# RWKV-6 attention and an erf-gated MLP on one core: products of near tokens over blocks of 16 instead of 8

## The chip, the cores and the metric

The kernel runs on one core of a Trainium2 chip. A core has TensorE (matmul), VectorE, ScalarE, GpSimd and SyncE; in the profile they are PE (and PEld, the loading of weights), DVE, ACT, POOL and SP. The metric is the device time of one execution in microseconds (us), the median of several runs. The profile is of one further execution; its span is 635.4 us.

## The reference

Everything is float32. The first half is a recurrent attention over batch 4, 8 heads, 768 tokens and head size 48:

```python
for t in range(S):
    kt, vt, rt, wt = (k[:, :, t], v[:, :, t], r[:, :, t], w[:, :, t])
    cur = np.einsum('bhd,bhe->bhde', u[None] * kt, vt)
    y[:, :, t] = np.einsum('bhd,bhde->bhe', rt, state + cur)
    state = wt[:, :, :, None] * state + np.einsum('bhd,bhe->bhde', kt, vt)
```

So token t reads token s < t with the weight sum over d of r[t] * k[s] * w[s+1] * ... * w[t-1], and itself with r * u * k. The heads' outputs, side by side, are the 3072 x 384 input x of the second half:

```python
h = x @ w_in                                  # 384 -> 2048
sp = np.maximum(h, 0.0) + np.log1p(np.exp(-np.abs(h)))
g = h * erf(sp)
return (g @ w_out).astype(np.float32)         # 2048 -> 384
```

## The kernel before

**Steps.** The tokens go through in 12 steps. A step handles 128 tokens of two batch entries, all 8 heads: 16 pairs of head and batch entry, in chunks of 64 tokens (HC = 64, two chunks to a step). `attend` (line 350) is the attention of one step, `hidden` (L520) and `project` (L559) are the layers w_in and w_out of a step, cut into 8 pieces each. A piece of `project` is 4 matmuls of 384 columns (L568), a piece of `hidden` 6 of 256 columns (L547); each float32 matmul is two instructions in the profile. Step s runs its own attention beside `project` of step s-3 and `hidden` of step s-1. After step 11 only dense pieces are left.

**Levels.** Within a chunk of 64 tokens, pairs (s, t) are covered by six levels. Level n takes the pairs in which s lies in the left and t in the right half of a block of 2^n tokens. For a level, TensorE multiplies the columns of r and k of 32 blocks (L390) into the PSUM tile `pp`; then VectorE scales r and k in place by products of decays (`scale`, L226, the instruction at L231), so that the next level has the right decay between halves, and copies the level's pairs from `pp` into the matrix `own` (L409, a copy under a mask; at level six ScalarE does it, L416). Products of decays over blocks of 2, 4, ... tokens (`tots`) come from GpSimd (L306). The next level's matmuls wait for the scaling before them.

**After the levels.** TensorE multiplies `own` with v into y (L435, in two halves), transposes k (L446, which needs level six's scaling), and forms the chunk's update of the state (L464). VectorE adds it to the decayed state, which is `middle`, the state between the two chunks (L476); GpSimd decays that (L480) and VectorE makes the next state (L484). Then TensorE adds what y reads from the state and from `middle` (L498). ScalarE copies y into xT, the input of w_in, and the next step begins.

**Near tokens.** Steps 0 to 3 run all six levels on TensorE. From step 4 on (DIRECT = 4), levels one to three are replaced: `prepare(s)` (L235) computes all pairs within blocks of 8 tokens (NEAR = 8) by elementwise work. It needs r, k and w a second time, as rows: a partition holds a block of 8 tokens of two heads, 96 numbers per token. GpSimd multiplies, distance by distance (n = 0 to 7): terms[n] = r[n:] * k[:-n] (L296), and between two distances k is carried on by k *= w (L295). The terms lie in two rooms of SBUF, `front` and `back`. VectorE sums them over the head (L324), the sums go to DRAM and come back in the order of tokens (`by_blocks`, `by_tokens`), and VectorE puts them on the block diagonal of `own` (L342). The levels from four on then overwrite the rest.

**Order.** Every engine works in the order in which the program is written; the order is set by hand. `prepare` is a generator. During step s, `attend` advances the generator of step s+1 by `next(following)` after every level above NEAR_LOG, after the transposes and before the last place; in step 3, the first that prepares near tokens for a successor, this is so too:

```python
if level > (NEAR_LOG if s >= DIRECT - 1 else 1):
    next(following, None)
place(level - 1)
```

The first advance issues all products and the decay products on GpSimd; the third issues the sums and both DRAM transfers on VectorE and SyncE; the fourth and the rest the scalings one to three and `own`. `place` puts the dense pieces and the activations between the levels: `advance` (L585) issues the next of softplus (L529), erf (L532) and the multiplication h * erf (L536), `beside` (L594) the pieces. In step 3, two pieces go to each of eight places, `project` at the first four and `hidden` at the last four. From step 4 on there are five places with 4 and 4 pieces of `project` and 3, 3 and 2 of `hidden`. At the end of a step the inputs and the rows of step s+2 are loaded (`load_step`, `load_rows`). Steps 0 to 3 also convert the weights (`convert`).

Of the kernel before, what the change touches and what calls it, by code (L numbers as in the profile page):

```python
# [11 lines left out]
FP32 = mybir.dt.float32  # L12
# [3 lines left out]
ALU = mybir.AluOpType  # L16

P = 128
# [3 lines left out]
NJ = 2  # L22
# [11 lines left out]


DIRECT = 4
NEAR_LOG = 3
NEAR = 1 << NEAR_LOG
LOG = 6
MASKED = 5  # L40
# [2 lines left out]
def view(ap, offset, dims):  # L43

    return bass.AP(ap.tensor, ap.offset + offset, [ap.ap[0], *dims])
# [12 lines left out]
def kernel(  # L58
# [14 lines left out]
    nc = tc.nc  # L73
    PSUM = bass.MemoryType.PSUM

    n_steps, _, _, JP, C = rkw.shape
    NH, D = v.shape[2:]
# [9 lines left out]
    assert n_steps == SPC * n_pairs and NP == KT + 1 == 4 and NG == 2 and P // NEAR * NH // 2 == P  # L87
# [23 lines left out]
    first = const.tile([P, HC], FP32, name="first")  # L111
    block_sb = const.tile([P, HC], FP32, name="block_sb")

    sums = const.tile([P, NEAR, 2, NEAR], FP32, name="sums")
    u_row = const.tile([P, 2 * D], FP32, name="u_row")
# [110 lines left out]
    def scale(s, level):  # L226

        in_t, tots = loaded[s][0], ready[s][1]
        half, nb = 1 << (level - 1), JP * C >> level
        halves = view(in_t[:, 0:2], half, [[JP * C - half, 2], [2 * half, nb], [1, half]])  # L230
        nc.vector.tensor_mul(  # L231
            halves, halves, view(tots[level - 1], 0, [[1, 2], [2, nb], [0, half]])
        )

    def prepare(s):  # L235


        in_t = loaded[s][0]
        if s < DIRECT:
            rk1 = att.tile([P, 2, JP, C], FP32, name="rk1", bufs=1)  # L240
            parts = 1 if s else NJ
            def multiply_u(i, x):
                n = slice(i * JP // parts, (i + 1) * JP // parts)
                with_u, plain = (
                    [
                        t[:, x, n].rearrange("p n (t two) -> p n t two", two=2)[..., one]
                        for t in (rk1, in_t)
                    ]
                    for one in (x, 1 - x)
                )  # L250
                if not s and not x:
                    nc.vector.tensor_mul(
                        with_u[0], with_u[1],
                        u_sb[:, :, None].to_broadcast([P, NP, C // 2]),
                    )
                    nc.vector.tensor_copy(out=plain[0], in_=plain[1])
                    return
                for p in range(NP):
                    of = slice(p, None, NP)
                    nc.scalar.mul(  # L260
                        out=with_u[0][:, of], in_=with_u[1][:, of], mul=u_sb[:, p : p + 1]
                    )
                nc.scalar.copy(plain[0], plain[1])

            if s < 2:
                for i in range(parts):
                    for x in range(2):
                        multiply_u(i, x)
                yield
            else:  # L270
                yield
                yield
                multiply_u(0, 0)
        if s >= DIRECT:
# [4 lines left out]
            room = [front[:].rearrange("p x n t -> p (x n t)")] + [  # L279
                back[:].rearrange("p x n two -> p (x n two)").bitcast(FP32)  # L280
            ]
            terms = []
            for n in range(NEAR):
                if n in (0, 3):
                    free, used = room.pop(0), 0
                size = (NEAR - n) * 2 * D
                terms.append(free[:, used : used + size].rearrange("p (t n) -> p t n", n=2 * D))
                used += size
            nc.gpsimd.tensor_mul(  # L289
                terms[0], k, u_row[:, None, :].to_broadcast([P, NEAR, 2 * D])  # L290
            )
            nc.gpsimd.tensor_mul(terms[0], terms[0], r)
            for n in range(1, NEAR):
                if n > 1:
                    nc.gpsimd.tensor_mul(k[:, : NEAR - n], k[:, : NEAR - n], w[:, n - 1 : NEAR - 1])  # L295
                nc.gpsimd.tensor_mul(terms[n], r[:, n:], k[:, : NEAR - n])  # L296

        tots, tot = [], in_t[:, 2].rearrange("p n t -> p (n t)")
        tot_sb = att.tile([P, JP * (C - NC)], FP32, name="tot_sb")
        used = 0  # L300
        for level in range(1, LOG + 1):
            tots.append(tot)
            nb = JP * C >> level
            new = tot_sb[:, used : used + nb]
            pair = tot.rearrange("p (n two) -> p n two", two=2)
            nc.gpsimd.tensor_mul(new, pair[:, :, 0], pair[:, :, 1])  # L306
            tot = new
            used += nb
            if level == 2 and s < DIRECT:
                yield  # L310
        if s < DIRECT:
            ready[s] = rk1, tots, tot
            yield
            if s >= 2:
                yield
                multiply_u(0, 1)
            return

        own = att.tile([P, NH, HC], FP32, name="own")
        ready[s] = own, tots, tot  # L320
        yield
        yield
        for n in range(NEAR):
            nc.vector.tensor_reduce(  # L324
                out=view(sums[:], n, [[2 * NEAR + 1, NEAR - n], [NEAR, 2]]),
                in_=terms[n].rearrange("p t (n d) -> p t n d", d=D),
                axis=mybir.AxisListType.X, op=ALU.add,
            )
        by_blocks = dram.tile([P, NEAR, 2 * NEAR], FP32, name="by_blocks")
        nc.sync.dma_start(out=by_blocks[:], in_=sums[:].rearrange("p s n t -> p s (n t)"))  # L330
        by_tokens = att.tile([P, NH, NEAR], FP32, name="by_tokens", bufs=1)
        nc.sync.dma_start(
            out=by_tokens[:].rearrange("p (g n) t -> p g (n t)", n=2),
            in_=by_blocks[:].rearrange("(g b) s n -> (b s) g n", g=NH // 2),
        )
# [13 lines left out]

    def attend(s, xT, place, behind):  # L350
# [243 lines left out]
    def beside(s, k):  # L594


        kind, of, pieces = (projs, s - 3, 2) if k < 4 else (hids, s - 1, 2)
        if s >= DIRECT:
            kind, of = (projs, s - 3) if k < 2 else (hids, s - 1)
            pieces = (4, 4, 3, 3, 2)[k]  # L600
        if s in ALONE:
            kind, of, pieces = hids, s - 1, 1
        if not 0 <= of < n_steps:
# [3 lines left out]
        for _ in range(pieces):  # L607
            next(kind[of])


    CONVERT = (
# [13 lines left out]
    with tc.manual_schedule(  # L625
# [19 lines left out]
        for s in range(n_steps):  # L645
            xTs[s] = xs.tile([P, KT, UNIT], FP32, name="xT")
            places = iter(range(8))

            def convert_at(n):
                if s < len(CONVERT) and n < len(CONVERT[s]):  # L650
                    for what in CONVERT[s][n]:
                        conversion.send(what)

            def place(n):
                if s in ALONE:
                    convert_at(n)
                    advance(ALONE[s][n])
                else:
                    advance()
                    convert_at(n)  # L660
                beside(s, next(places))

            attend(s, xTs[s], place, lambda: convert_at(LOG + 2))
            if s + 2 < n_steps:
                load_step(s + 2)
                if s + 2 >= DIRECT:
# [101 lines left out]
```

## Time and profile before

The median of three runs is 637.16 us (637.15 to 637.78).

| engine | busy us | share of the span | instructions |
|---|---|---|---|
| PE | 622.5 | 98% | 7338 |
| PEld | 458.2 | 72% | 7338 |
| DVE | 306.9 | 48% | 311 |
| ACT | 301.3 | 47% | 374 |
| POOL | 276.1 | 43% | 240 |

A group of instructions in the profile is read as: source line, engine, operation, output <- input by the program's names, shapes, count | busy us in all, mean ns of one | us that the engine sat idle just before, and what ended most of that. A row of the timeline is: start in us, length in us, then the same names; "x64" says that 64 instructions are merged. In brackets stands the idle time before it and what released it. A group of matmuls that overlap has a mean of one that is longer than its share of the busy time: 2816 instructions of L390 with a mean of 214 ns take 46.5 us in all. The TensorE clock that the throttle granted is 1.00 throughout.

In the steps from 4 to 10 the three compute engines beside TensorE have time left: in the step from 207.23 to 256.10 us, VectorE is busy for 24.8 us, ScalarE for 21.8 and GpSimd for 27.6 of 48.9.

### The profile page before, as it was taken

What the parts mean: (1) busy time and instruction counts of PE and PEld (TensorE: products, weight loads), DVE (VectorE), ACT (ScalarE), POOL (GpSimd) and SP (SyncE); (2) the same over time, 40 slices, a digit from 0 to 9 for tenths busy, and PEclk for the clock granted to TensorE, in tenths of its full rate; (3) what the DMA queues carried; (4) which work ended last, traced back from release to release, by engine and by line L of the source; (5) the groups of instructions that cost most, each with busy time, mean ns of one, the idle gap of its engine ahead of it and who ended that gap; (6) DMA issues with size and microseconds to landing.
All of it is one profiled execution on the core that took longest, in us unless ns stands there. A gap on an engine that the chain in (4) does not pass through costs nothing.

```text
span 635.4 us, 16193 instructions
## 1 busy us (share of the span) xinstructions
PE 622.5 (98%) x7338; PEld 458.2 (72%) x7338; DVE 306.9 (48%) x311; ACT 301.3 (47%) x374; POOL 276.1 (43%) x240
## 2 busy tenths in 40 slices
PE   8889999999999999999999999999999999999997
PEld 7567787678678678668668668768768758768654
DVE  4588597577346256266265365366446322011110
ACT  2537778756424544544534524624624625634520
POOL 4338175495194196097097087088079100000000
PEclk9999999999999999999999999999999999999999
DMA  8366371400500500500510410420330000000000
GB/s 326 130 241 201 136 260 56 200 15 10 206 26 10 207 26 9 206 26 10 183 49 10 168 65 9 152 81 9 103 128 11 8 13 14 7 23 3 1 25 25
DMA packets 24628, 53.84 MB, mean 85 GB/s; under 512 B 11376, under 2 KB 16752, under 8 KB 23152
## 3 DMA queue, kind: packets, MB, share of 16 engines
q1 hardware_dynamic: 23408, 52.23, 23.1%
q8 instruction: 57, 0.93, 0.6%
q10 hardware_dynamic: 1152, 0.59, 0.4%
q14 instruction: 11, 0.09, 0.1%
HBM read 46.39 MB, written 5.24 MB: 81 GB/s over the span
## 4 chain that ended last, share of the span: by engine, by line
PE 91%; DVE 3%; ACT 3%; issue 1%; DMA 1%; POOL 0%; SPq 0%; DVEq 0%; ACTq 0%
PE m L568 40%; PE m L547 38%; PE pp L390 6%; PE y L435 2%; PE pp L446 2%; PE y L498 2%; PE pp L464 2%; DVE in L231 1%; DMA in<-in_rkw 1%; ACT rk L260 1%; DVE own L409 1%; ACT own L416 0%; ACT rest L189 0%; ACT pp L187 0%; DMA xT<-y 0%
## 5 line engine op out<-in xcount | busy, mean ns | idle before, releaser
L547 PE MATMUL m<-xT,w_in_sb 128*128 128x256 f32 x1152 | 260.1, 382 | 0.6 <-DMA xT<-y 0.3
L568 PE MATMUL m<-w_out_sb,h 128*128 128x384 f32 x768 | 253.5, 489 | 0.0
L547 PEld LDWEIGHTS m<-xT,w_in_sb 128*128 128x128 f32 x1152 | 214.6, 190 | 33.2 <-issue 1.6
L568 PEld LDWEIGHTS m<-w_out_sb,h 128*128 128x128 f32 x768 | 144.2, 190 | 97.4
L231 DVE TENSOR_TENSOR in<-in,tot_sb 128x1024 f32<-128x1024 f32 x60 | 80.8, 1347 | 154.4 <-PE pp L390 153.2
L536 DVE TENSOR_TENSOR h<-h,sp 128x1024 f32<-128x1024 f32 x48 | 80.3, 1713 | 67.7 <-ACT sp L532 67.7
L554 ACT COPY h<-m 128x512 f32<-128x512 f32 x96 | 56.2, 586 | 104.2 <-PE m L547 104.0
L577 ACT COPY o<-m 128x384 f32<-128x384 f32 x24 | 11.5, 479 | 148.4 <-PE m L568 136.6
L289 POOL TENSOR_TENSOR rk<-words,u_row 128x768 f32<-128x768 f32 x8 | 17.3, 2157 | 124.8 <-DMA words<-in_rk_rows 124.8
L306 POOL TENSOR_TENSOR tot_sb<-tot_sb 128x256 f32<-128x256 f32 (+4 forms) x60 | 54.1, 902 | 4.5
L390 PEld LDWEIGHTS pp<-in 48*64 48x64 f32 (+1 forms) x2816 | 41.0, 127 | 20.5 <-issue 17.5
L295 POOL TENSOR_TENSOR words<-words,rest 128x576 f32<-128x576 f32 (+5 forms) x48 | 52.6, 1096 | 3.8
L390 PE MATMUL pp<-in 48*64 48x64 f32 (+1 forms) x2816 | 46.5, 214 | 4.2 <-DVE own L409 2.3
L532 ACT ACTIVATE sp<-sp 128x2048 f32<-128x2048 f32 x24 | 45.9, 1911 | 0.3
L529 ACT ACTIVATE sp<-h 128x2048 f32<-128x2048 f32 x24 | 45.9, 1911 | 0.3
L532 ACT ACT_TABLE_LOAD x24 | 30.8, 1283 | 20.4 <-issue 20.2
L296 POOL TENSOR_TENSOR words<-words 128x480 f32<-128x480 f32 (+4 forms) x40 | 32.8, 819 | 3.1
L529 ACT ACT_TABLE_LOAD x24 | 30.8, 1283 | 3.0 <-issue 2.6
L296 POOL TENSOR_TENSOR rk<-words 128x672 f32<-128x672 f32 (+1 forms) x16 | 31.9, 1994 | 0.6
L324 DVE TENSOR_REDUCE sums<-words 128x10 f32<-128x480 f32 (+4 forms) x40 | 17.7, 452 | 26.5 <-POOL words L296 25.9
L203 POOL TENSOR_TENSOR w_out_sb<-w_out_sb,rest 128x768 int32<-128x768 int32 x8 | 18.1, 2271 | 27.4 <-DVE w_out_sb L199 27.4
L476 DVE TENSOR_TENSOR middle<-faded,pp 48x384 f32<-48x384 f32 x20 | 11.0, 552 | 32.9 <-PE pp L464 32.6
(57 smaller groups left out, 427.2 us busy)
## 6 DMA issues: line engine op xcount, KB each, us to landing
in<-in_rkw SPq DMA_DIRECT2D x11, 1536.0 KB, 6.6
words<-in_moe_w_in SPq DMA_DIRECT2D x8, 768.0 KB, 6.0
words<-in_moe_w_out SPq DMA_DIRECT2D x8, 768.0 KB, 4.8
words<-in_rk_rows SPq DMA_DIRECT2D x8, 768.0 KB, 8.4
v<-in_v SPq DMA_DIRECT2D x12, 384.0 KB, 7.0
out<-o SPq DMA_DIRECT2D x24, 192.0 KB, 1.9
rest<-in_w_rows SPq DMA_DIRECT2D x8, 384.0 KB, 8.9
in<-in_rkw SPq DMA_DIRECT2D x2, 512.0 KB, 4.6
```

The costliest lines, as they stand in the source:

```text
L203: nc.gpsimd.tensor_tensor(out=into, in0=into, in1=rest[:], op=ALU.add)
L231: nc.vector.tensor_mul(halves, halves, view(tots[level - 1], 0, [[1, 2], [2, nb], [0, half]]))
L295: nc.gpsimd.tensor_mul(k[:, : NEAR - n], k[:, : NEAR - n], w[:, n - 1 : NEAR - 1])
L296: nc.gpsimd.tensor_mul(terms[n], r[:, n:], k[:, : NEAR - n])
L306: nc.gpsimd.tensor_mul(new, pair[:, :, 0], pair[:, :, 1])
L390: nc.tensor.matmul(pp[s0 : s0 + m, e, n, :m], lhsT=rk[rows(e), 1, n, s0 : s0 + m], rhs=rk[rows(e), 0, n, t0 : t0 + m], start=True, stop=True,)
L529: nc.scalar.activation(held[0][:], h[:], AF.Softplus)
L532: nc.scalar.activation(held[0][:], held[0][:], AF.Erf)
L536: nc.vector.tensor_mul(h[:, part], h[:, part], held[0][:, part])
L547: nc.tensor.matmul(ps[:, ff, :], lhsT=w_in_sb[:, g * FG + f + ff, kk * P : (kk + 1) * P], rhs=xT[:, kk, :], start=kk == 0, stop=kk == KT - 1,)
L554: nc.scalar.copy(h[:, f : f + FT, :], ps[:])
L568: nc.tensor.matmul(ps[j][:], lhsT=gs[g][:, f, j * C : (j + 1) * C], rhs=w_out_sb[:, g * FG + f, :], start=g + f == 0, stop=g == NG - 1 and ...
```

## The change

Blocks of near tokens grow from 8 to 16 (NEAR_LOG 3 to 4), so that level four also leaves TensorE in steps 4 to 11. A partition now holds 16 tokens of one head, 48 numbers per token. There are 16 distances instead of 8. The work on them is divided: VectorE multiplies the distances 0 to 4 and carries k up to distance 5 (NEARER = 5), and sums these five at once; GpSimd multiplies distances 5 to 15, and VectorE sums them later. The rooms for the terms are used twice. Since VectorE now needs the rows at the start of a step, they are loaded one step earlier in program order, at level six. As level four no longer has a place for dense pieces, the order of pieces and activations in steps 4 and later is written out in `in_order`, and y3 has one buffer instead of two. The purpose is to take work from TensorE, the busiest engine, and give it to engines that have time left.

```diff
-NEAR_LOG = 3
+NEAR_LOG = 4
+NEARER = 5
...
-            nc.gpsimd.tensor_mul(
-                terms[0], k, u_row[:, None, :].to_broadcast([P, NEAR, 2 * D])
-            )
-            nc.gpsimd.tensor_mul(terms[0], terms[0], r)
-            for n in range(1, NEAR):
-                if n > 1:
-                    nc.gpsimd.tensor_mul(k[:, : NEAR - n], k[:, : NEAR - n], w[:, n - 1 : NEAR - 1])
-                nc.gpsimd.tensor_mul(terms[n], r[:, n:], k[:, : NEAR - n])
+            for room, distances in (
+                (front, range(1, 4)), (back, (0, 4)), (front, range(5, 9)), (back, range(9, NEAR))
+            ):
...
         own = att.tile([P, NH, HC], FP32, name="own")
         ready[s] = own, tots, tot
+        nc.vector.tensor_mul(terms[0], k, u_row[:, None, :].to_broadcast([P, NEAR, D]))
+        nc.vector.tensor_mul(terms[0], terms[0], r)
+        for n in range(1, NEARER):
+            nc.vector.tensor_mul(terms[n], r[:, n:], k[:, : NEAR - n])
+            carry(nc.vector, n + 1)
+        for n in range(NEARER):
+            sum_up(n)
+        for n in range(NEARER, NEAR):
+            nc.gpsimd.tensor_mul(terms[n], r[:, n:], k[:, : NEAR - n])
+            carry(nc.gpsimd, n + 1)
         yield
         yield
-        for n in range(NEAR):
-            nc.vector.tensor_reduce(
...
+        for n in range(NEARER, NEAR):
+            sum_up(n)
+        by_blocks = dram.tile([P, NEAR, NEAR], FP32, name="by_blocks")
+        nc.sync.dma_start(out=by_blocks[:], in_=sums[:])
...
+        for level in range(1, NEAR_LOG):
+            scale(s, level)
         yield
-        scale(s, 1)
-        scale(s, 2)
-        yield
-        scale(s, 3)
+        scale(s, NEAR_LOG)
...
-        y3 = att.tile([P, UNIT], FP32, name="y3")
+        y3 = att.tile([P, UNIT], FP32, name="y3", bufs=1)
...
+    def in_order(s, k):
+        for what in ("APPPAPP", "APPPHH", "AHHH", "AHHH")[k]:
+            if what == "A":
+                advance()
+            elif what == "P":
+                piece(projs, s - 3)
+            else:
+                piece(hids, s - 1)
...
             def place(n):
+                if n == LOG - 1 and DIRECT - 1 <= s < n_steps - 2:
+                    load_rows(s + 2)
+                if s >= DIRECT:
+                    in_order(s, next(places))
+                    return
...
-        for k in range(15):
-            advance()
-            beside(n_steps + k // 5, k % 5)
+        for k in range(12):
+            in_order(n_steps + k // 4, k % 4)
```

In the changed kernel, VectorE's products and first sums of step s+1 are issued by the first advance, which now comes after level five of step s.

More of the change, by code (lines that the diff above doesn't have):

```diff
@@ L86 @@
     assert C == P == NC * HC and HC == 1 << LOG and NE == 2 and D <= EP and NP * NE * D == DM == KT * P
-    assert n_steps == SPC * n_pairs and NP == KT + 1 == 4 and NG == 2 and P // NEAR * NH // 2 == P
+    assert n_steps == SPC * n_pairs and NP == KT + 1 == 4 and NG == 2 and P // NEAR * NH == P
     const = ctx.enter_context(tc.tile_pool(name="const", bufs=1))
@@ L112 @@
     block_sb = const.tile([P, HC], FP32, name="block_sb")
-    sums = const.tile([P, NEAR, 2, NEAR], FP32, name="sums")
-    u_row = const.tile([P, 2 * D], FP32, name="u_row")
+    sums = const.tile([P, NEAR, NEAR], FP32, name="sums")
+    u_row = const.tile([P, D], FP32, name="u_row")
     w_in_sb = const.tile([P, NT, DM], FP32, name="w_in_sb")
@@ L278, in prepare, with sum_up, carry @@
             back = wide.tile([P, 2, DM, 2], I32, name="words", bufs=3)
[L279 to L282, printed above, removed]
-            for n in range(NEAR):
[L284 to L289, printed above, removed]
-                terms[0], k, u_row[:, None, :].to_broadcast([P, NEAR, 2 * D])
-            )
-            nc.gpsimd.tensor_mul(terms[0], terms[0], r)
-            for n in range(1, NEAR):
-                if n > 1:
-                    nc.gpsimd.tensor_mul(k[:, : NEAR - n], k[:, : NEAR - n], w[:, n - 1 : NEAR - 1])
-                nc.gpsimd.tensor_mul(terms[n], r[:, n:], k[:, : NEAR - n])
+            front = front[:].rearrange("p x n t -> p (x n t)")
+            back = back[:].rearrange("p x n two -> p (x n two)").bitcast(FP32)
+            terms = {}
+            for room, distances in (
+                (front, range(1, 4)), (back, (0, 4)), (front, range(5, 9)), (back, range(9, NEAR))
+            ):
+                used = 0
+                for n in distances:
+                    size = (NEAR - n) * D
+                    terms[n] = room[:, used : used + size].rearrange("p (t d) -> p t d", d=D)
+                    used += size
+            def sum_up(n):
+                nc.vector.tensor_reduce(
+                    out=view(sums[:], n, [[NEAR + 1, NEAR - n]]), in_=terms[n],
+                    axis=mybir.AxisListType.X, op=ALU.add,
+                )
+            def carry(engine, n):
+                if 1 < n < NEAR:
+                    engine.tensor_mul(
+                        k[:, : NEAR - n], k[:, : NEAR - n], w[:, n - 1 : NEAR - 1]
+                    )
         tots, tot = [], in_t[:, 2].rearrange("p n t -> p (n t)")
@@ L320, in prepare @@
         ready[s] = own, tots, tot
+        nc.vector.tensor_mul(terms[0], k, u_row[:, None, :].to_broadcast([P, NEAR, D]))
[8 more added lines that the diff above has]
+            carry(nc.gpsimd, n + 1)
         yield
         yield
-        for n in range(NEAR):
-            nc.vector.tensor_reduce(
[L325 to L330, printed above, removed]
+        for n in range(NEARER, NEAR):
+            sum_up(n)
+        by_blocks = dram.tile([P, NEAR, NEAR], FP32, name="by_blocks")
+        nc.sync.dma_start(out=by_blocks[:], in_=sums[:])
         by_tokens = att.tile([P, NH, NEAR], FP32, name="by_tokens", bufs=1)
         nc.sync.dma_start(
-            out=by_tokens[:].rearrange("p (g n) t -> p g (n t)", n=2),
-            in_=by_blocks[:].rearrange("(g b) s n -> (b s) g n", g=NH // 2),
-        )
+            out=by_tokens[:], in_=by_blocks[:].rearrange("(g b) s t -> (b s) g t", g=NH)
+        )
+        for level in range(1, NEAR_LOG):
+            scale(s, level)
         yield
-        scale(s, 1)
-        scale(s, 2)
-        yield
-        scale(s, 3)
+        scale(s, NEAR_LOG)
         nb = HC // NEAR
@@ L597, in beside, with piece @@
         kind, of, pieces = (projs, s - 3, 2) if k < 4 else (hids, s - 1, 2)
-        if s >= DIRECT:
-            kind, of = (projs, s - 3) if k < 2 else (hids, s - 1)
-            pieces = (4, 4, 3, 3, 2)[k]
         if s in ALONE:
             kind, of, pieces = hids, s - 1, 1
+        for _ in range(pieces):
+            piece(kind, of)
+    def piece(kind, of):
         if not 0 <= of < n_steps:
@@ L606, in beside @@
             kind[of] = hidden(xTs[of], gated[of]) if kind is hids else project(of, gated[of])
-        for _ in range(pieces):
-            next(kind[of])
+        next(kind[of])
+    def in_order(s, k):
[6 more added lines that the diff above has]
+                piece(hids, s - 1)
     CONVERT = (
@@ L665 @@
                 load_step(s + 2)
-                if s + 2 >= DIRECT:
+                if s + 2 == DIRECT:
                     load_rows(s + 2)
-        for k in range(15):
-            advance()
-            beside(n_steps + k // 5, k % 5)
+        for k in range(12):
+            in_order(n_steps + k // 4, k % 4)
 def level_masks():
@@ L711, in by_blocks @@
     def by_blocks(x):
-        x = x.reshape(B // NJ, NJ, NP // 2, 2, 2, n_pairs, P // NEAR, NEAR, D).transpose(
-            5, 0, 4, 1, 2, 6, 7, 3, 8
+        x = x.reshape(B // NJ, NJ, NP, 2, n_pairs, P // NEAR, NEAR, D).transpose(
+            4, 0, 3, 1, 2, 5, 6, 7
         )
@@ L718 @@
     u_rows = np.broadcast_to(
-        u.reshape(NP // 2, 2, 2, D).transpose(2, 0, 1, 3)[:, None, :, None],
-        (2, NJ, NP // 2, P // NEAR, 2, D),
+        u.reshape(NP, 2, D).transpose(1, 0, 2)[:, None, :, None], (2, NJ, NP, P // NEAR, D)
     )
@@ L753 @@
         "in_w_rows": by_blocks(w),
-        "in_u_rows": np.ascontiguousarray(u_rows).reshape(P, 2 * D),
+        "in_u_rows": np.ascontiguousarray(u_rows).reshape(P, D),
     }
```

## The prediction

> **What bounds the kernel now.** I read the page first: busy times, then the chain that ended last.
>
> ```profile
> PE 622.5 (98%) x7338; PEld 458.2 (72%) x7338; DVE 306.9 (48%) x311; ACT 301.3 (47%) x374; POOL 276.1 (43%) x240
> PE 91%; DVE 3%; ACT 3%; issue 1%; DMA 1%; POOL 0%; SPq 0%; DVEq 0%; ACTq 0%
> PE m L568 40%; PE m L547 38%; PE pp L390 6%; PE y L435 2%; PE pp L446 2%; PE y L498 2%; PE pp L464 2%; DVE in L231 1%; DMA in<-in_rkw 1%; ACT rk L260 1%; DVE own L409 1%; ACT own L416 0%; ACT rest L189 0%; ACT pp L187 0%; DMA xT<-y 0%
> ```
>
> TensorE is the bound: what leaves its row is gained, and whatever makes it wait is lost, because the tail after step 11 is only dense layers and cannot give time back. Next, the timeline of TensorE in a repeating step (columns: start us, duration us):
>
> ```profile
> 353.74 1.11 PE L390 MATMUL pp<-in 48*64 48x64 f32 x64
> 354.78 10.59 PE L568 MATMUL m<-w_out_sb,h 128*128 128x384 f32 x32
> 365.30 1.16 PE L390 MATMUL pp<-in 48*64 48x64 f32 x64
> 366.39 10.59 PE L568 MATMUL m<-w_out_sb,h 128*128 128x384 f32 x32
> 376.91 0.76 PE L390 MATMUL pp<-in 48*32 48x32 f32 x64
> 402.57 1.11 PE L390 MATMUL pp<-in 48*64 48x64 f32 x64
> ```
>
> Levels four, five and six start at 353.74, 365.30 and 376.91, and the next step at 402.57: 48.83 us without a hole. From start to start a 64-row level costs 1.04 to 1.09 us. Last, all engines in step 3, the first to prepare near tokens for a successor (step 4):
>
> ```profile
> 122.62 1.82 POOL L289 TENSOR_TENSOR rk<-words,u_row 128x768 f32<-128x768 f32 x1
> 131.44 1.16 PE L390 MATMUL pp<-in 48*64 48x64 f32 x64
> 132.67 2.03 DVE L231 TENSOR_TENSOR in<-in,tot_sb 128x1024 f32<-128x1024 f32 x1 [0.31 <-PE pp L390]
> 134.62 0.73 DVE L409 COPY_PREDICATED own<-mask_sb,pp 128x512 f32<-128x512 int32 x1
> 144.56 1.09 PE L446 MATMUL pp<-ident,in 128*128 128x128 f32 x8
> 151.84 1.14 DVE L476 TENSOR_TENSOR middle<-faded,pp 48x384 f32<-48x384 f32 x2 [1.42 <-PE pp L464]
> 157.95 0.63 PE L498 MATMUL y<-in,middle 48*48 48x64 f32 x32
> 158.39 1.11 PE L390 MATMUL pp<-in 48*64 48x64 f32 x64
> ```
>
> GpSimd begins its products at 122.62, while TensorE is at level three. Level five starts at 131.44, step 4 at 158.39: only 26.95 us of TensorE work lie between, because 8 of step 3's 16 dense pieces stand before level five. In steps 4 and later of the changed kernel level five comes first, with all 16 behind it. I write T for us after 131.44.
>
> [...] both are slowed by part rather than one fully: the pair at L536 takes 2.36 us alone at 615.20, but 4.78 here.
>
> ```profile
> 417.20 2.68 POOL L292 TENSOR_TENSOR rk<-rk,words 128x768 f32<-128x768 f32 x1
> 418.73 4.78 DVE L536 TENSOR_TENSOR h<-h,sp 128x1024 f32<-128x1024 f32 x2
> 376.29 1.41 POOL L296 TENSOR_TENSOR rk<-words 128x576 f32<-128x576 f32 x1
> 386.64 0.39 POOL L295 TENSOR_TENSOR words<-words,rest 128x96 f32<-128x96 f32 x1
> 1.68 7.67 PE L630 MATMUL m<-ident 128*128 128x128 f32 x40 [1.68 <-POOL ident masks.py:199]
> ```
>
> [...] 40 warm-up matmuls span 7.6 us, while the equal transposes (L446) run 8 in 0.92, so 40 would take 4.6: a cold start costs about 3.0 us.
>
> **The change, part by part.**
>
> *Level four off TensorE.* Eight steps lose one level of 64 rows and the switches around it. Adding pieces: before, 1.04+10.52+1.09+10.52+0.68, then 3, 3 and 2 pieces of w_in; after, 1.04+13.15+0.68+7.89, then 2, 3 and 3. The pieces are the same 16, so a step falls from 48.8 to about 47.7: 1.1 us, **8.8 us in eight steps**. The new order of pieces, the extra place for an activation and y3 with one buffer cost nothing: ScalarE is busy 21.8 us of a step and finishes each before its reader.
>
> *New work on VectorE, per step:* ten products of 768, 768, 720, 672, 672, 624, 624, 576, 576 and 528 elements. [...] Then five sums (L324: 0.945 us for 768, 0.842 for 672), 3.8 us. All stand in VectorE's queue directly behind level five's copy, and ahead of level six's scaling.
>
> *GpSimd, per step:* 21 products, 5808 elements. Start to start, L295 and L296 take 0.47 us for 96 elements and 1.48 for 576, so 0.25 us + 2.14 ns per element: 5.25 + 12.4 = 17.7 us. Before it was 15 instructions with 6240 elements, 17.1. But they start only when VectorE has carried k to distance five and read its first two sums. Three VectorE products (3.7 us alone) run beside them; from 126.3 to 135.8 GpSimd lost 3.6 us to 4.8 us of such work, 0.75 each, so 2.75 more.
>
> *A repeating step* (0 at its level five). VectorE's ten products: 3.2 to 11.8. The step's inputs land near 10, the decay products follow, GpSimd multiplies from 14.3 to 34.8. VectorE's eleven late sums trail it to 35.0; scalings one to three to 39.1; the activation's product 41.5; middle 42.6; S_next 44.7; scaling four 45.9. TensorE wants middle at 47.3 and scaling four at 47.7. Hidden, but with 1.8 us to spare.
>
> *Step 3.* VectorE ends level five at T 3.2, its products at 11.8, its sums at 15.6. Scaling six follows at 17.6 (contended 2.0), while TensorE reaches the transposes at 13.1: it waits 4.5. GpSimd runs from 13.6 to 13.6+17.7+2.75 = 34.0. The late sums end at 34.3. Behind them in VectorE's queue stand scalings one to three (38.4), then middle (39.6), S_next after GpSimd's 0.95 (41.7), scaling four (43.0). TensorE, out of work at 31.1 even with the first wait, needs middle for y and scaling four for step 4's level five: step 4 starts at T 43.05 instead of 26.95, **16.1 us lost, once**.
>
> *The clock.* TensorE then idles 8 us, runs 0.6 us and idles 3 more. If the clock falls, step 4 begins cold. [...] the start suggests 3.0. I take 2.5.
>
> *Loads.* Rows come a step earlier; the row wait of GpSimd, 124.8 us in all (L289), goes but delayed nobody. The transposition through DRAM has 2048 runs of 64 bytes instead of 1024. Landing took 2.2 us; even at 4 it ends by 42 in the repeating step, before its reader at 45.9. Nothing.
>
> Sum: 637.2 - 8.8 + 16.1 + 2.5 = **647.0 us**.
>
> **The rivals.** (a) Step 3 hides the preparation: 637.2 - 8.8 = 628.4. For it: every later step does. Against: VectorE's queue in step 3 puts middle behind sums that wait for GpSimd, and 39 us do not fit in 27. (b) The repeating steps stall as well: were GpSimd 4 us slower in each (its contended instructions take 2.6 us rather than 1.8), scaling four would come 2.2 us late in seven of them: 647.0 + 15 = 662. For it: the small spare. Against: the long new VectorE products run while GpSimd mostly waits[...]. (c) The stall is not much over half of what I add up (9 us) and the clock stays: 637.2 - 8.8 + 9 = 637.4, no change. For it: scalings and sums could run faster uncontended, 3 us in all. Against: GpSimd's 17.7 us are measured rates, and nothing in the queue shortens them.
>
> **How the numbers follow.** Forecast 0.77, spread from 642 to 652 by the clock [...] and contention (2 us either way); (a) 0.07; (b) 0.09; (c) 0.07. The range 640 to 655 leaves out (a), most of (b) and part of (c). Slower: forecast, (b) and most of (c), 0.90; within 0.2% 0.03; faster 0.07.
>
> **What would show it.** Right: in the changed kernel's timeline TensorE has holes before step 3's transposes (about 4 us), before the matmul that reads middle (about 8) and before step 4's level five (about 3), released by VectorE; the repeating steps last 47.7 us with no holes; GpSimd's products start about 13 us after level five. The clock shows as slower L568 matmuls at the start of step 4. Wrong: step 3 from level five to its end lasts 27 us, or repeating steps show a wait for scaling four.

## The result, and the profile after

The changed kernel takes 644.69 us (median of four runs, 644.45 to 645.41), the kernel before 637.17 us beside it (637.15 to 637.78). The ratio is 1.0117, with a 95% interval of 1.0100 to 1.0135: slower by 7.5 us. The forecast was 647.0, range 640 to 655. Line numbers of the changed kernel are higher than those of before: L403 the levels, L581 w_out, L560 w_in, L232 the scalings, L448 y from `own`, L459 the transposes, L511 y from the state, L489 `middle`, L330, L331 and L333 VectorE's products, L338 GpSimd's, L302 the carrying of k by either engine, L294 the sums. The experiments move them by a few lines.

The page of the changed kernel, its busy times, its TensorE clock and its chain of work that ended last:

```profile
PE 617.7 (96%) x6826; PEld 455.0 (71%) x6826; DVE 399.1 (62%) x447; ACT 301.4 (47%) x374; POOL 254.5 (40%) x288
PEclk9999999997799999999999999999999999999999
PE 85%; DVE 6%; POOL 3%; issue 2%; ACT 2%; DMA 1%; SPq 0%; DVEq 0%; POOLq 0%; ACTq 0%
```

TensorE has 512 instructions and 4.8 us of busy time less, as meant. But the profiled span grew from 635.4 to 642.6 us, so TensorE now stands still for 24.9 us instead of 12.9. VectorE and GpSimd, 3% of the chain before, hold 9% of it, and the clock dips in two of the 40 slices, those from 144.6 to 176.7 us.

The timeline of TensorE in the changed kernel, from level five of step 3 to the start of step 6 (start us, length us, idle time before it in brackets):

```profile
131.49 1.16 PE L403 MATMUL pp<-in 48*64 48x64 f32 x64
...
144.03 0.67 PE L448 MATMUL y<-own,v 64*48 64x64 f32 x32
148.59 1.97 PE L459 MATMUL pp<-ident,in 128*128 128x128 f32 x8 [3.90 <-DVE in L232]
150.35 7.22 PE L560 MATMUL m<-xT,w_in_sb 128*128 128x256 f32 x24
...
164.19 0.66 PE L511 MATMUL y<-in,s 48*48 48x64 f32 x32
170.17 1.68 PE L511 MATMUL y<-in,middle 48*48 48x64 f32 x32 [5.32 <-DVE middle L489]
174.08 1.99 PE L403 MATMUL pp<-in 48*64 48x64 f32 x64 [2.23 <-DVE in L232]
176.00 14.16 PE L581 MATMUL m<-w_out_sb,h 128*128 128x384 f32 x40
...
223.49 1.11 PE L403 MATMUL pp<-in 48*64 48x64 f32 x64
...
271.04 1.11 PE L403 MATMUL pp<-in 48*64 48x64 f32 x64
```

Step 4 starts at 174.08, 42.59 us after level five of step 3; before it was 26.95. That is a loss of 15.64 us, in one place. The three waits are where the forecast put them, and VectorE ends all three. After 223.49 the step starts are 271.04, 318.58 and so on, each 47.55 us after the last, against 48.83 before. The tail of dense layers takes 86.2 us in both kernels (from 556.40 here, from 549.17 before).

What VectorE and GpSimd do in those 42.6 us, from the timeline of all engines:

```profile
142.33 0.71 DVE L302 TENSOR_TENSOR words<-words,rest 128x528 f32<-128x528 f32 x1
...
144.85 1.33 POOL L338 TENSOR_TENSOR rk<-words 128x528 f32<-128x528 f32 x1 [18.98 <-PE m L560]
...
146.76 1.77 DVE L232 TENSOR_TENSOR in<-in,tot_sb 128x1024 f32<-128x1024 f32 x1
...
148.45 4.26 DVE L549 TENSOR_TENSOR h<-h,sp 128x1024 f32<-128x1024 f32 x2
...
164.98 0.28 POOL L338 TENSOR_TENSOR words<-words 128x48 f32<-128x48 f32 x1
...
165.30 0.20 DVE L294 TENSOR_REDUCE sums<-words 128x1 f32<-128x48 f32 x1 [0.47 <-POOL words L338]
...
169.57 1.13 DVE L489 TENSOR_TENSOR middle<-faded,pp 48x384 f32<-48x384 f32 x2
...
172.80 1.23 DVE L232 TENSOR_TENSOR in<-in,tot_sb 128x1024 f32<-128x1024 f32 x1
```

VectorE's last product ends at 143.0, GpSimd's first begins at 144.85 and its last ends at 165.26; only then come the last of VectorE's sums of GpSimd's products (the late sums, below), `middle`, and scaling four (172.80), on which step 4's level five waits. The releaser shown at 144.85 is misleading: the matmul named had long been done. What ended just then is VectorE's second sum (one of the three merged from 143.82 on), which frees the room in SBUF that GpSimd's product writes.

The granted clock in the changed kernel by stretches (the number before the DMA share, which is second from the right):

```profile
148.00:152.00 4.00, 3.41 (x12) 3.09 (x13) 4.00 (x3) 1.39 (x2) 3.84 (x3) 0.50 0.02 4
170.00:174.00 4.00, 1.54 (x32) 1.12 (x32) 2.98 (x6) 1.20 (x4) 0.83 (x1) 0.50 0.00 0
174.00:178.00 4.00, 3.92 (x67) 2.97 (x68) 2.99 (x4) 2.79 (x2) 0.00 (x0) 0.50 0.61 166
```

The 0.50 in all three rows says that after the waits of 3.90 and 5.32 us TensorE ran at half clock for some us ("cold", below); from 156 to 160 us, and from 178 to 182, it was at 1.00 again.

The end of a repeating step, from the timeline of all engines:

```profile
363.03 1.23 DVE L232 TENSOR_TENSOR in<-in,tot_sb 128x1024 f32<-128x1024 f32 x1
...
366.13 1.11 PE L403 MATMUL pp<-in 48*64 48x64 f32 x64
```

Scaling four ends at 364.26, the level that reads it starts at 366.13 and didn't wait: 1.87 us to spare.

### The profile page after: what moved, and what is told of

It reads as the page before. It is cut to its first block, busy times and chain, and to the rows that moved or that the text cites. A ratio compares the mean times of both kernels' runs of the same rounds, so it can differ in the third digit from the quotient of the medians.

```text
span 642.6 us, 15381 instructions
## 1 busy us (share of the span) xinstructions
PE 617.7 (96%) x6826; PEld 455.0 (71%) x6826; DVE 399.1 (62%) x447; ACT 301.4 (47%) x374; POOL 254.5 (40%) x288
## 4 chain that ended last, share of the span: by engine, by line
PE 85%; DVE 6%; POOL 3%; issue 2%; ACT 2%; DMA 1%; SPq 0%; DVEq 0%; POOLq 0%; ACTq 0%
PE m L581 39%; PE m L560 34%; PE pp L403 5%; DVE in L232 2%; PE y L448 2%; PE pp L459 2%; PE y L511 2%; PE pp L477 1%; POOL words L302 1%; POOL rk L338 1%; DMA in<-in_rkw 1%; POOL words L338 1%; DVE own L422 1%; DVE sums L294 1%; DVE words L302 0%
## 5 line engine op out<-in xcount | busy, mean ns | idle before, releaser
L560 PE MATMUL m<-xT,w_in_sb 128*128 128x256 f32 x1152 | 261.2, 383 | 0.6 <-DMA xT<-y 0.3
L581 PE MATMUL m<-w_out_sb,h 128*128 128x384 f32 x768 | 254.5, 490 | 0.0
L560 PEld LDWEIGHTS m<-xT,w_in_sb 128*128 128x128 f32 x1152 | 217.0, 191 | 35.1 <-issue 1.6
L581 PEld LDWEIGHTS m<-w_out_sb,h 128*128 128x128 f32 x768 | 144.7, 191 | 97.7 <-issue 0.9
L549 DVE TENSOR_TENSOR h<-h,sp 128x1024 f32<-128x1024 f32 x48 | 73.6, 1574 | 59.6 <-ACT sp L545 59.6
L232 DVE TENSOR_TENSOR in<-in,tot_sb 128x1024 f32<-128x1024 f32 x60 | 82.1, 1368 | 40.5 <-PE pp L403 39.6
L302 POOL TENSOR_TENSOR words<-words,rest 128x480 f32<-128x480 f32 (+4 forms) x80 | 67.6, 845 | 6.3
L294 DVE TENSOR_REDUCE sums<-words 128x16 f32<-128x768 f32 (+8 forms) x72 | 33.3, 463 | 52.0 <-POOL words L338 52.0
L338 POOL TENSOR_TENSOR rk<-words 128x528 f32<-128x528 f32 (+3 forms) x32 | 51.7, 1615 | 23.5 <-PE m L560 19.0
L315 POOL TENSOR_TENSOR tot_sb<-in 128x512 f32<-128x512 f32 x12 | 14.9, 1244 | 110.3 <-DMA in<-in_rkw 110.3
L403 PEld LDWEIGHTS pp<-in 48*64 48x64 f32 (+1 forms) x2304 | 33.6, 128 | 18.6 <-issue 10.9
L590 ACT COPY o<-m 128x384 f32<-128x384 f32 x24 | 11.5, 479 | 72.4 <-PE m L581 72.2
L403 PE MATMUL pp<-in 48*64 48x64 f32 (+1 forms) x2304 | 38.1, 215 | 6.5 <-DVE in L232 2.9
L294 DVE TENSOR_REDUCE sums<-rk 128x15 f32<-128x720 f32 (+6 forms) x56 | 37.3, 713 | 10.3 <-POOL rk L338 10.3
L338 POOL TENSOR_TENSOR words<-words 128x336 f32<-128x336 f32 (+6 forms) x56 | 33.2, 593 | 4.4
L429 ACT COPY own<-pp 32x512 f32<-32x512 f32 x24 | 13.8, 575 | 44.2 <-PE pp L403 43.9
L315 POOL TENSOR_TENSOR tot_sb<-tot_sb 128x256 f32<-128x256 f32 (+4 forms) x60 | 31.4, 523 | 4.5
```

Source lines behind the costliest of these rows:

```text
L232: nc.vector.tensor_mul(halves, halves, view(tots[level - 1], 0, [[1, 2], [2, nb], [0, half]]))
L294: nc.vector.tensor_reduce(out=view(sums[:], n, [[NEAR + 1, NEAR - n]]), in_=terms[n], axis=mybir.AxisListType.X, op=ALU.add,)
L302: engine.tensor_mul(k[:, : NEAR - n], k[:, : NEAR - n], w[:, n - 1 : NEAR - 1])
L403: nc.tensor.matmul(pp[s0 : s0 + m, e, n, :m], lhsT=rk[rows(e), 1, n, s0 : s0 + m], rhs=rk[rows(e), 0, n, t0 : t0 + m], start=True, stop=True,)
L549: nc.vector.tensor_mul(h[:, part], h[:, part], held[0][:, part])
L560: nc.tensor.matmul(ps[:, ff, :], lhsT=w_in_sb[:, g * FG + f + ff, kk * P : (kk + 1) * P], rhs=xT[:, kk, :], start=kk == 0, stop=kk == KT - 1,)
```

## The experiments

The theory: the loss is a debt paid once, because step 3 has too little work left behind its level five for a preparation that begins there; the repeating steps gain. Rivals: the near tokens' work slows every step (contention, GpSimd too slow); the early loading of rows costs something; the debt can't be avoided but only moves.

**GpSimd's share left out of the preparation for step 4.** In step 3 the distances 5 to 15 are neither multiplied nor summed.

```diff
-        for n in range(NEARER, NEAR):
+        for n in range(NEARER, NEAR) if s > DIRECT else ():
             nc.gpsimd.tensor_mul(terms[n], r[:, n:], k[:, : NEAR - n])
...
-        for n in range(NEARER, NEAR):
+        for n in range(NEARER, NEAR) if s > DIRECT else ():
             sum_up(n)
```

> In step 3 alone, the preparation of step 4 leaves out GpSimd's products of distances 5 to 15 and their sums (so step 4 lacks these pairs); all later steps are whole. Stall theory (the loss is made once, in step 3, by GpSimd's products between VectorE's first sums and middle): the holes before the matmul that reads middle and before step 4's level five all but vanish, the one before the transposes (about 4 us, made by VectorE's products) stays, the clock stays up: 644.7 - 11 - 2 = 632. Rival, load of the repeating steps (the loss comes from VectorE and GpSimd blocking each other there): at most 1 us less than 644.7.

> The same kernel as the first of these experiments (step 4 lacks the pairs at distances 5 to 15), for a profile of an undisturbed run: 632, one hole of about 4 us before step 3's transposes and none over 1.5 us behind it.

Measured: 0.9921 of before (0.9905 to 0.9938), and, run again, 632.1 us or 0.9918 (0.9903 to 0.9934). TensorE's timeline in the second run:

```profile
133.04 1.16 PE L403 MATMUL pp<-in 48*64 48x64 f32 x64
...
149.57 1.97 PE L459 MATMUL pp<-ident,in 128*128 128x128 f32 x8 [3.34 <-DVE in L232]
...
165.04 1.11 PE L403 MATMUL pp<-in 48*64 48x64 f32 x64
...
212.59 1.11 PE L403 MATMUL pp<-in 48*64 48x64 f32 x64
```

The two waits behind the late sums are gone, and step 4 is not cold: it lasts 47.55 us. Step 4 starts 32.0 us after level five, 10.6 earlier than in the changed kernel; with the 1.86 us that step 4 lost to the clock this makes 12.5 us, and the medians lie 12.6 apart. (The run of this trace took 633.5 us; it reached level five 1.5 us later than the changed kernel's trace did.) What stays is 5.05 us over before: the wait of 3.34 for scaling six, which stands behind VectorE's own ten products and five sums, and the slowed matmuls after it (granted clock 0.63 from 150 to 154 us). So GpSimd's products, with the late sums behind them, add about two thirds of the stall (10.6 of 15.64) to the third that VectorE's early work makes alone.

**The rows alone.** The kernel before, with only the rows loaded at level six.

```diff
             def place(n):
+                if n == LOG - 1 and DIRECT - 1 <= s < n_steps - 2:
+                    load_rows(s + 2)
...
-                if s + 2 >= DIRECT:
+                if s + 2 == DIRECT:
                     load_rows(s + 2)
```

> The kernel before with one part of the change alone: rows are loaded at level six for the step after next. Both theories that put the loss elsewhere: no change, 637.2, since the time that GpSimd waits for rows delays nobody; GpSimd's products start about 12 us earlier in the repeating steps. Rival, the gain of 1.28 us in a repeating step comes in part from the earlier rows: 634 to 636.

Measured: 637.28 us, ratio 1.0000 (0.9991 to 1.0009). GpSimd's timeline, first of the kernel before, then of this one:

```profile
366.78 2.66 POOL L289 TENSOR_TENSOR rk<-words,u_row 128x768 f32<-128x768 f32 x1 [17.54 <-DMA words<-in_rk_rows]
```

```profile
349.56 1.82 POOL L289 TENSOR_TENSOR rk<-words,u_row 128x768 f32<-128x768 f32 x1
```

GpSimd's first product comes 17 us earlier and nobody gains or loses by it. The loading is not the cause.

**TensorE kept at work.** If the waits cost twice, once as waiting and once as a lower clock, matmuls without use in the waits give back the second part alone. `stay_warm` issues matmuls of 512 columns whose result nobody reads, before the transposes, before the matmul that reads `middle`, and before step 4's level five.

```diff
+        if s == DIRECT:
+            stay_warm(3)
         for level in range(NEAR_LOG + 1 if s >= DIRECT else 1, LOG + 1):
...
+        if s == DIRECT - 1:
+            stay_warm(4)
         ps = products([P, JP, P])
...
+            if h and s == DIRECT - 1:
+                stay_warm(9)
```

> Idle TensorE time of step 3 is filled with dummy matmuls (7 of 512 columns before the transposes, 16 before the matmul that reads middle, 6 before step 4's level five), nothing else. Stall theory: step 4 still starts about 42.6 us after level five of step 3, but warm: its level five takes 1.05 us instead of 1.92 and the next five pieces of w_out 13.1 instead of 14.1, so 644.7 - 1.9 = 642.8. Clock rival (most of the 17.5 us lost in steps 3 and 4 is the lowered clock): 635 or less.

> The filling again, with lengths that fit the holes (a dummy matmul of 512 columns takes 0.87 us, twice what was reckoned): 4 before the transposes, 9 before the matmul that reads middle, 3 before step 4's level five. Stall theory: step 4 starts 42.6 us after level five of step 3 as without filling, but warm: 644.7 - 1.9 = 642.8. Clock rival: 635 or less.

The first of the two used 7, 16 and 6 matmuls in place of 4, 9 and 3: 652.07 us, ratio 1.0234 (1.0219 to 1.0249), a miss, because a matmul of 512 columns takes nearly 0.9 us, twice what I had reckoned, and the filling itself held up step 4. The second, with the numbers of the diff, took 642.85 us, ratio 1.0087 (1.0074 to 1.0101), as expected. Its TensorE timeline:

```profile
131.80 1.16 PE L405 MATMUL pp<-in 48*64 48x64 f32 x64
...
162.38 7.99 PE L389 MATMUL m<-in,ident 128*128 128x512 f32 x18
...
174.42 1.16 PE L405 MATMUL pp<-in 48*64 48x64 f32 x64
175.51 13.17 PE L587 MATMUL m<-w_out_sb,h 128*128 128x384 f32 x40
```

Step 4 still starts 42.62 us after level five (42.59 without filling), though TensorE ran at full clock all the way (1.00 from 150.0 to 174.4): its slow matmuls inside step 3 cost nothing, since VectorE's chain sets the end. What comes back is in step 4: level five 1.09 us instead of 1.92 from start to start, five pieces of w_out 13.10 instead of 14.09. The clock is worth 1.8 us of the loss, and no more.

**Work moved behind level five.** Step 3 takes one piece at each of its first four places, so that twelve of the sixteen, not eight, stand behind level five.

```diff
+                if s == DIRECT - 1:
+                    advance()
+                    convert_at(n)
+                    k = next(places)
+                    for what in ("P", "P", "P", "P", "PPP", "PHH", "HHH", "HHH")[k]:
+                        piece(*((projs, s - 3) if what == "P" else (hids, s - 1)))
+                    return
```

> The changed kernel with step 3's 16 dense pieces in another order: 1, 1, 1, 1, 3, 3, 3, 3 over its eight places instead of 2 each, so four pieces (10.6 us) more lie behind its level five. Stall theory: the wait of step 3 falls from 15.6 to about 5.5 us, half before middle and half before step 4's level five, the clock stays up: 644.7 - 10.5 - 1.9 = 632.3. Rival, load of the repeating steps: 644.7 as before, because no work is taken away.

Measured: 637.98 us, ratio 1.0012 (1.0005 to 1.0019): 6.7 us better than the changed kernel, some 5.7 short of what was expected. TensorE's timeline:

```profile
119.36 1.16 PE L403 MATMUL pp<-in 48*64 48x64 f32 x64 [1.15 <-DVE in L232]
...
123.22 1.16 PE L403 MATMUL pp<-in 48*64 48x64 f32 x64
...
163.19 0.32 PE L511 MATMUL y<-in,middle 48*48 48x64 f32 x4 [2.87 <-DVE middle L489]
...
167.10 1.99 PE L403 MATMUL pp<-in 48*64 48x64 f32 x64 [2.67 <-DVE in L232]
```

Level five comes 8.3 us earlier, not 10.6: with one piece between levels, level four waits 1.15 us for its scaling, and level three 0.95 us for one of VectorE's copies into `own`. The chain behind it is 43.9 us long, 1.3 more than before the move, and two waits remain at its end, after which the clock has fallen again (0.50 from 168 to 172 us). The wait before the transposes is gone. The mechanism holds (level five 8.3 us earlier, step 4 7.0 us earlier), the sum of its terms was too hopeful.

**Scalings ahead of the late sums.** If only VectorE's queue holds the scalings back, they can run while GpSimd multiplies.

```diff
         yield
         yield
+        for level in range(1, NEAR_LOG + 1):
+            scale(s, level)
         for n in range(NEARER, NEAR):
             sum_up(n)
...
-        for level in range(1, NEAR_LOG):
-            scale(s, level)
         yield
-        scale(s, NEAR_LOG)
```

> The changed kernel with one order altered: the scalings one to four of the next step stand ahead of VectorE's late sums instead of behind them. Stall theory, with its step that the tail of the late sums (scalings, middle, S_next, scaling four) is what TensorE waits for at the end of step 3: scaling four is no longer in the tail, but GpSimd is blocked 3.7 us more, so step 4 starts about 3 us earlier, 641.6; repeating steps stay at 47.55. Rival (the wait ends with GpSimd alone and the order behind it does not matter): 644.7 or, with the added blocking, 648.

Measured: 643.0 us, ratio 1.0091 (1.0077 to 1.0104). Timeline of all engines:

```profile
154.09 2.12 DVE L232 TENSOR_TENSOR in<-in 128x1024 f32<-128x1024 f32 x1
...
156.31 5.64 DVE L232 TENSOR_TENSOR in<-in,tot_sb 128x1024 f32<-128x1024 f32 x3
...
169.87 0.28 POOL L338 TENSOR_TENSOR words<-words 128x48 f32<-128x48 f32 x1
```

TensorE's timeline:

```profile
132.94 1.16 PE L402 MATMUL pp<-in 48*64 48x64 f32 x64
...
172.96 2.01 PE L402 MATMUL pp<-in 48*64 48x64 f32 x62
```

The four scalings, now beside GpSimd's products, take 7.8 us, where behind the late sums three took 4.2 and the fourth 1.2. GpSimd is slowed in turn (384 elements in 1.86 us instead of 1.00) and ends 37.2 us after level five instead of 33.8. Step 4 starts 40.0 us after level five, 2.6 earlier than in the changed kernel. Without GpSimd's 3.4 us it would have been about 6 (an estimate), so contention costs somewhat more than half of the gain; a slower cold start (five pieces in 14.89 us) takes back another 0.8.

**Both, and step 4's late sums after the next state.** This combines the last two edits, puts the first decay of the state ahead of the levels on GpSimd, and moves step 4's own late sums and `own` behind the next state in VectorE's queue.

```diff
+        for level in range(1, NEAR_LOG + 1):
+            scale(s, level)
+        if s == DIRECT:
+            yield
         for n in range(NEARER, NEAR):
             sum_up(n)
...
+        if c:
+            nc.gpsimd.tensor_mul(
+                faded[0][:], S[:], ends[:, :, 0:1].to_broadcast([P, JP, D])
+            )
         for level in range(NEAR_LOG + 1 if s >= DIRECT else 1, LOG + 1):
```

> The changed kernel with pieces 1, 1, 1, 1, 3, 3, 3, 3 in step 3, the scalings ahead of the late sums, the decay of the old state first in each step on GpSimd, and step 4's late sums behind the state update. Stall theory: nothing that TensorE reads in step 3 is behind GpSimd's products any more, so the holes before middle and before step 4's level five close and only the 2 us between the early levels stay: 644.7 - 15.6 - 1.9 + 2.4 = 629.6, and up to 3 us more if step 4 starts with its own preparation late. Rival, load of the repeating steps: not under 640.

Measured: 637.3 us, ratio 0.9999 (0.9991 to 1.0007). Timeline of all engines, the last line from TensorE's own:

```profile
160.74 1.11 PE L409 MATMUL pp<-in 48*64 48x64 f32 x64
...
162.68 1.12 DVE L499 TENSOR_TENSOR s<-faded,pp 48x384 f32<-48x384 f32 x2 [8.00 <-POOL faded L495]
...
172.70 1.23 DVE L357 TENSOR_TENSOR own<-block_sb,by_tokens 128x1024 f32<-128x1024 f32 x1 [4.84 <-DMA by_tokens<-by_blocks]
...
195.02 1.97 PE L465 MATMUL pp<-ident,in 128*128 128x128 f32 x8 [5.44 <-DVE in L232]
...
216.02 1.11 PE L409 MATMUL pp<-in 48*64 48x64 f32 x64
```

Behind its level five (123.38) step 3 no longer waits; step 4 starts 37.4 us after it. But the debt moved on. VectorE makes the next state only after a wait of 8.00 us for GpSimd's decay of `middle`, which still stands behind GpSimd's products. Then it has step 4's late sums to do (4.0 us), waits 4.84 us for them to come back from DRAM, and so begins the products for step 5 only 15.0 us after step 4's level five (175.71), not 3. TensorE waits 5.44 us before step 4's transposes and then runs at half clock (0.50 from 195 to 199 us), and step 4 takes 55.28 us. Its 7.7 us over the usual 47.55 are the whole gap to the 629.6 of the forecast. From the next step on, 47.55 again. This supports the rival that the debt only moves, as long as step 4 is to have blocks of 16.

**A smaller debt: step 4 with blocks of 8.** If the debt comes from preparing too much in step 3, then step 4 can be prepared as in the kernel before (near tokens in blocks of 8, all products on GpSimd, level four on TensorE), and step 4, which has 15 of its 16 pieces behind level five, prepares the first blocks of 16, for step 5. All else is as in the changed kernel. Nothing is left out.

```diff
+def near_log(s):
+    return SHORT_LOG if s == DIRECT else NEAR_LOG
...
-        for level in range(NEAR_LOG + 1 if s >= DIRECT else 1, LOG + 1):
+        for level in range(near_log(s) + 1 if s >= DIRECT else 1, LOG + 1):
...
-            if level > (NEAR_LOG if s >= DIRECT - 1 else 1):
+            if level > (near_log(s + 1) if s >= DIRECT - 1 else 1):
                 next(following, None)
...
+        if s == DIRECT:
+            order = ("P", "APPAPP", *order[1:])
```

> The changed kernel, but step 4, the first with near tokens, keeps blocks of 8 and its level four on TensorE: its preparation in step 3 is that of the kernel before (all products on GpSimd from level three on, 17 us of GpSimd instead of VectorE's 12 and GpSimd's 18 in a row). Blocks of 16 from step 5 on. Stall theory: step 3 is as short as before (26.95 us from level five to step 4), seven steps save 1.28 us, and step 4 loses 0.8 because one piece stands before its level five: 637.2 - 9.0 + 0.8 = 629.0. Rival, load of the repeating steps (steps 5 to 11 have it all): 643 or more. Debt rival (whichever step begins the blocks of 16 pays the 12 us, as the two reorderings of step 3 paid them): 640 or more.

Measured: 628.65 us (628.51 to 628.83), ratio 0.9857 (0.9843 to 0.9872). It beats both kernels. TensorE's timeline:

```profile
158.73 1.11 PE L464 MATMUL pp<-in 48*64 48x64 f32 x64
159.78 2.85 PE L642 MATMUL m<-w_out_sb,h 128*128 128x384 f32 x8
162.56 1.16 PE L464 MATMUL pp<-in 48*64 48x64 f32 x64
...
207.90 1.16 PE L464 MATMUL pp<-in 48*64 48x64 f32 x64
...
255.49 1.11 PE L464 MATMUL pp<-in 48*64 48x64 f32 x64
```

Step 4 starts at 158.73, as in the kernel before, without a wait. It takes 49.17 us, 0.34 more than a step before, and prepares blocks of 16 behind a level five at 162.56. That is almost in time: scaling four for step 5 ends at 207.85, 45.3 us after level five, and step 5 starts at 207.90, some 0.3 us later than TensorE's own work would have let it. The steps after it take 47.55 each (the first 47.59). So the first preparation of the larger blocks, which cost 15.64 us where 26.95 us of work lay behind level five, costs 0.3 where some 45 do. With the share left out above this shows the cause, and also that the debt could be avoided after all, by putting the switch one step later.

**How much a repeating step can bear.** Extra products on GpSimd (480 numbers a partition), ahead of its first, in the preparation for steps 5 to 11; once one, once three.

```diff
+        for _ in range(3 if s > DIRECT else 0):
+            nc.gpsimd.tensor_mul(
+                own[:].rearrange("p n t -> p (n t)")[:, : 10 * D].rearrange("p (t d) -> p t d", d=D),
+                r[:, :10], r[:, :10],
+            )
```

> The changed kernel with one extra GpSimd product of 480 elements (1.28 us, written where the step's own matrix is written over later) before its products, in the preparation of steps 5 to 11. Stall theory: a repeating step has 1.9 us to spare between scaling four and the next level five, so nothing changes: 644.7. Rival, load of the repeating steps: every us on GpSimd is paid seven times, 653.7.

> As the last, with three such products (3.85 us). Stall theory: 3.85 - 1.9 = 1.95 us late in seven steps, 658.4, with TensorE waiting for scaling four at each level five. Rival, load of the repeating steps: 671.6. If GpSimd's time were hidden throughout: 644.7.

With one: 644.43 us, ratio 1.0117 (1.0095 to 1.0139), hidden (644.69 without it). With three: 650.03 us, ratio 1.0189 (1.0174 to 1.0204), 5.3 us over the changed kernel where 13.7 were expected. The timeline of all engines with three:

```profile
333.90 3.12 POOL L338 TENSOR_TENSOR own<-words 128x480 f32<-128x480 f32 x3
...
357.22 0.29 POOL L343 TENSOR_TENSOR words<-words 128x48 f32<-128x48 f32 x1
...
367.32 1.23 DVE L232 TENSOR_TENSOR in<-in,tot_sb 128x1024 f32<-128x1024 f32 x1
...
368.60 1.16 PE L408 MATMUL pp<-in 48*64 48x64 f32 x64 [0.80 <-DVE in L232]
```

This step began at 320.02. The three took 3.12 us, not 3.85, and GpSimd ends 37.49 us after level five, 2.85 later than in the changed kernel (34.64 in the step from 318.58). With 1.87 to spare that makes 0.98, and the step takes 48.58 us, 1.03 more than 47.55. So the spare time is measured, and the size of the load was wrong. Nor does every step pay alike: the six steps from 223.18 to 513.32 take 48.36 on average, the one after the longest 47.92. When level five is late, the step's own inputs land earlier against it (GpSimd's first product of decays starts 8.56 us after the level five at 272.10, against 9.63 after the one at 271.04 in the changed kernel), which pays a part back.

## Why the prediction was right, by its steps

| term | predicted us | measured us |
|---|---|---|
| level four off TensorE, eight steps | -8.8 | -10.3 |
| stall in step 3 | +16.1 | +15.64 |
| clock, step 4 | +2.5 | +1.86 |
| spare time in a repeating step | 1.8 | 1.87 |
| loading rows early | 0 | 0 |

The first three measured terms sum to 7.2 us, which is the difference of the two profiled spans; the forecast's sum to 9.8. All three erred to the same side, so none hid another.

*Level four.* A repeating step fell by 1.28 us, not 1.1. Of the 0.18 more, half lies ahead of the first piece of w_in: 22.67 us, where I had 1.04+13.15+0.68+7.89 = 22.76 (the five pieces took 13.10 and the three 7.84). The other half lies in the rest of the step: 24.88 us against 24.98 before, which I had held equal. Step 4 has the same gain hidden under its cold start: 49.41 us, where it took 47.55 when it was not cold (GpSimd's share left out), hence 10.3 for eight steps with the clock's 1.86 apart.

*The stall.* Counted in us after level five (131.49), the forecast against the measurement: VectorE's products end at 11.8 and 11.5, GpSimd's begin at 13.6 and 13.4 and end at 34.0 and 33.8, scaling four ends at 43.0 and 42.5. The forecast's length for VectorE's ten products, 8.6 us (from 3.2 to 11.8), was an estimate; they took 8.56 (134.48 to 143.04). VectorE's five early sums were put at 3.8 us, though the lengths given for them add up to about 4.2; start to start they took 3.80. The mechanism, the queue of VectorE, was right at every link, and the skipped share and the blocks of 8 in step 4 confirm it by experiment. How the waiting is divided was less right. I had 4.5, 8 and 3 us of waits. From start to start, against before, TensorE lost 3.97 before the transposes, 2.70 in slowed transposes and pieces, 5.49 before the matmul that reads `middle` and 3.47 up to level five. The waits themselves are 3.90, 5.32 and 2.23 us: the clock had fallen after the first (0.50 from 148 to 152 us), which the forecast didn't foresee, and the slowed work filled part of what would have been waiting. The sum doesn't care, as the filling experiment shows.

*The clock.* The direction was right and the size below my value of 2.5, which was an estimate from the first 40 matmuls of the kernel before. That a fallen clock slowed those was not shown: the granted clock there is 1.00 from 0 to 9 us. Nor does that profile show a fall in a wait: TensorE's longest after the first matmul is 1.3 us. In step 3 a single wait of 3.34 us was enough for a fall (GpSimd's share left out; granted clock 0.63 from 150 to 154 us), and so were 2.87 and 2.67 us with about 1 us of work between (one piece per place; 0.50 from 168 to 172 us).

*Contention.* I took 2.75 us of delay on GpSimd, and its end came within 0.2 of the forecast. In step 3 VectorE's pair at L549 took 4.26 us beside GpSimd and 2.35 where GpSimd had nothing to multiply (its share left out), while GpSimd's first product beside the sums took 1.33. The sums did not slow GpSimd where it can be compared: 288 elements at L338 took 0.81 us at 163.67 with the scalings first, with VectorE's sums running all the while, and 0.81 at 158.75 in the changed kernel, with VectorE idle. The forecast's reading that VectorE and GpSimd are both slowed by part, rather than one fully, misses what the ends show. From 148.5 us on VectorE and GpSimd finish by turns: 148.53, 149.59, 150.67, 151.64, 152.72, 153.67. VectorE's 1024 elements end 1.08 us after GpSimd's product before them (1.22 at 151.71 with GpSimd's share left out), GpSimd's 480 and 432 elements 1.06 and 0.95 to 0.97 us after VectorE's (where they were not slowed, 1.20 at 146.26 here and 1.10 at 344.83 with three extra products). My reading is that whole instructions took turns in these 5 us, with some 0.14 us of overlap, so that both engines looked slowed; the trace shows the ends and the lengths, not what holds an instruction back.

*Loads.* The sums came back through DRAM in 3.0 us (median; 2.2 before), and in the repeating step from 318.58 their reader (L355 at 364.17) didn't wait.

*The rivals.* That step 3 hides the preparation (628.4) is refuted by the 15.64 us. The version with blocks of 8 in step 4 came out at nearly the same number (628.65) by chance: there step 4 hides the preparation, and seven steps save 1.28 us, where this rival had eight with 1.1. That the repeating steps stall is refuted by 47.55 us in every one of them, and the load that it takes to make them stall is measured. A smaller stall with the clock unchanged is refuted by 15.64.

Not settled: why step 4's cold pieces differ between kernels with similar waits (14.09 us here, 14.89 with the scalings first).

## What to carry to other kernels

A change that moves work off the bounding engine pays in each iteration, but its pipeline must be filled once, and the first iteration that prepares for the new scheme may not have the slack of the others: read that one by itself in the timeline (here 15.64 us lost once against 1.28 gained per step). Write down the queue of the helping engine from the trigger to the last reader, and compare it with the work that stands behind the trigger. If it does not fit, move the switch to an iteration where it does, before reordering queues; filling the waits gave back only the clock here (1.8 us).

## What was unexpected of the hardware

- A float32 matmul of 128x512 takes 0.89 us on average (9 of them, 18 instructions, in 7.99 us); I had reckoned with half.
- GpSimd multiplied 480 numbers a partition by themselves in 1.04 us each, and took 1.20 for two different inputs of that size (L302 at 146.26 in the changed kernel).
- The time at half clock lay partly under the waiting and cost nothing there: of the slow matmuls only those after the last wait, 1.8 us (644.69 against 642.85), reached the end.
